# Reordering the TensorE stages of a round in a fused retention and adapter kernel

## The chip, the cores and the metric

The kernel runs on one core of one Trainium2 chip. The metric is device microseconds of one execution, lower is better. A core has five engines that each run their own list of instructions in order: TensorE (PE) for matmuls, VectorE (DVE), ScalarE (ACT), GpSimd (POOL) and SyncE (SP), which here issues nearly all transfers. [...]

## The reference

Two layers follow each other. The first is retention over q, k, v of shape (8 batches, 8 heads, 576 positions, 64): scores with a decay that depends on the distance, a causal mask, and the product with v.

```
scores = scale * matmul(q, k.transpose(0, 1, 3, 2))
ret    = scores * Dmat            # gamma_h ** (i - j) for i >= j, else 0
x      = matmul(ret, v)           # then (B, H, S, D) -> (B * S, H * D) = (4608, 512)
```

The second adds low-rank adapters to x: logits over 8 experts choose the two best for each token; their softmax weights scale the products with A (512 x 16 for each expert) and B (16 x 512).

```
logits = x @ w_gate               # (4608, 8), the top 2 chosen
delta += w * ((x @ A[e]) @ B[e])  # for the two chosen experts e
out    = x + delta
```

## The kernel before, in words

**Units.** The 576 positions are cut into four chunks of 128 and a last one of 64. A unit is one chunk of two batches (or the last chunk of four batches): units 0 to 15 are full, 16 and 17 hold the last chunk. A unit has 128 tokens in each of its two halves b. The decay is folded into q and k (scale_, on GpSimd, L166), and what earlier chunks contribute comes as a 64 x 64 state for each head, kept in the tiles blk.

**Stages of a unit on TensorE**, with the names that the profile shows for their outputs:

- T (L252): transposes of k (pt_k) and q (pt_q); evict_T copies them to kT and xq.
- SL and S (L355, L379): scores. S (ps_s) holds the first 64 keys against 128 queries, SL (a, L369) the second 64 keys against the second 64 queries. VectorE masks them: mask_e (L400) writes S's scores over xq, mask_l (L414) writes SL's to sl.
- U (L432): state products of k and v, in the other half of the tile a; add_state (L452) adds the old state.
- X (L464) and XL (L511): x, transposed, in the two banks px; X takes the masked S and the state, XL (the "late part") the masked SL. evict_x (L533) copies both to xT on ScalarE.
- Z (L563): x times the joined A and w_gate (pz). routing_1 copies it to zs on ScalarE, routing_2 finds the two best on VectorE, routing_3 makes the weights with two sigmoids on ScalarE (sg), routing_4 makes the weighted zc on GpSimd (cm, zc).
- P (L545): transposes zc (pzt); evict_z copies it to zT.
- B (L629): transposes xT into the banks po. Y (L656): adds zT times B to po. evict_o (L673) copies po to osb, which SP stores.

**Rounds.** The loop at L870 runs one round for each t from 3 on, and works on three units at a time: t, p = t - 1 and z = t - 2, besides the transposes of nxt = t + 1. The schedule is written out by hand: every engine works in the order in which the statements stand. A round of the kernel before gives TensorE SL(t), S(t), XL(p), U(t), X(p), the k transposes of nxt, B(z), the q transposes of nxt, P(z), Z(p), Y(z). So x of a unit is made one round after its scores. The rounds of t = 0 to 2 are written out ahead of the loop (L788 to L867), the work that is left after the last round stands behind it (L906 on).

**Banks.** The tiles in PSUM have tags. "s" and "a" are two banks each, "x0", "x1", "o0" and "o1" one each, which makes eight. In a round, "s" holds ps_s and then pt_k; "a" holds SL's and U's results and then pt_q; "x0" and "x1" hold px, then pz (x0) and pzt (x1); "o0" and "o1" hold po. A tag's next tile is written when the last one has been read.

**Transfers.** While clock["on"] holds, on_pe (L119) adds up an estimated duration of every matmul, and hangs the round's loads (of unit t + 3) and stores (of unit t - 3) on TensorE's instructions at set distances. The order of the engines' own work does not depend on these estimates.

Of the kernel before, what the change touches and what calls it, by code (L numbers as in the profile page):

```python
# [10 lines left out]
FP32 = mybir.dt.float32  # L11
# [7 lines left out]
def kernel(  # L19
# [441 lines left out]
                nc.vector.tensor_tensor(out=dst, in0=src, in1=old, op=ALU.add)  # L461


    def stage_X(u, bs=(0, 1)):  # L464
        c, bp = units[u]
        if u == NU - 1 and "px" not in st[u]:
            pa = pp.tile([128, 2, HP, 128], FP32, tag="a", name="pa")
            st[u]["px"] = [pa[:, 0], pp.tile([128, HP, 128], FP32, tag="x1", name="px1")]
        elif "px" not in st[u]:
            st[u]["px"] = [  # L470
                pp.tile([128, HP, 128], FP32, tag=f"x{b}", name=f"px{b}") for b in range(2)
            ]
        px = st[u]["px"]
        if c == 0:

            for hp in range(HP):
                for b in bs:
                    for ho in range(2):
                        on_pe(
                            52,  # L480
                            nc.tensor.matmul(
                                px[b][hf(ho), hp, :],
                                lhsT=blk(u)[hf(b), b, 2 * hp + ho, :],
                                rhs=facing(u, b, ho)[hf(b), hp, :],
                                start=False,
                                stop=True,
                                skip_group_check=True,
                            ),
                        )
            return  # L490
        full = c < NFULL
        parts = [(0, slice(0, 128))] if full else [(t, hf(t)) for t in range(2)]
        for b in bs:
            for hp in range(HP):
                for t, qc in parts:
                    bk = blk(u if full else 4 * NFULL + 2 * bp + t)
                    for ho in range(2):
                        on_pe(
                            107 if full else 60,
                            nc.tensor.matmul(  # L500
                                px[b][hf(ho), hp, qc],
                                lhsT=bk[:, b, 2 * hp + ho, :],
                                rhs=facing(u, b, ho)[:, hp, qc],
                                start=(hp == 0 and t == 0 and not full),
                                stop=True,
                                skip_group_check=True,
                            ),
                        )


    def stage_XL(u):  # L511
        px = st[u]["px"] = [
            pp.tile([128, HP, 128], FP32, tag=f"x{b}", name=f"px{b}") for b in range(2)
        ]
        sl = st[u]["sl"]
        vn, vl = nt(u, "v"), st[u]["vl"]
        for hp in range(HP):
            for b in range(2):
                for ho in range(2):
                    h, r = 2 * hp + ho, late_half(u, b)  # L520
                    on_pe(
                        29,
                        nc.tensor.matmul(  # L523
                            px[b][hf(ho), hp, 64:128],
                            lhsT=vn[64:128, b * H + h, :] if r else vl[0:64, h, :],
                            rhs=sl[hf(r), late_bank(u, b, ho), hp, :],
                            start=(hp == 0),
                            stop=False,
                            skip_group_check=True,
                        ),  # L530
                    )
# [55 lines left out]
    def routing_2(u):  # L587
        s = st[u]
        zs = s["zs"]
        m8 = mo.tile([128, 2, E], FP32, tag="m8", name="m8")  # L590
        ns = mo.tile([128, 2], FP32, tag="ns", name="ns")
        ge = mo.tile([128, 2, E], FP32, tag="ge", name="ge")
        for b in range(2):
            nc.vector.max(out=m8[:, b, :], in_=zs[:, b, ER : ER + E])  # L594
        nc.vector.scalar_tensor_tensor(
            out=ns, in0=m8[:, :, 0], scalar=-1.0, in1=m8[:, :, 1],
            op0=ALU.mult, op1=ALU.subtract,
        )
        nc.vector.tensor_tensor(
            out=ge, in0=zs[:, :, ER : ER + E],  # L600
            in1=m8[:, :, 1:2].broadcast_to((128, 2, E)), op=ALU.is_ge,
        )
        s["ns"], s["ge"] = ns, ge
# [22 lines left out]
            )  # L626
        s["zc"] = zc

    def stage_B(u, tag="o"):  # L629
        if tag == "s":  # L630
            both = st[u]["po2"] = pp.tile([128, 2, 2, HP, 64], FP32, tag="s", name="po")
            po = [both[:, ho] for ho in range(2)]
        else:
            po = [
                pp.tile([128, 2, HP, 64], FP32, tag=f"{tag}{ho}", name=f"po{ho}")
                for ho in range(2)
            ]
        for b in range(2):
            for dt in range(HP):
                for ho in range(2):  # L640
                    sl = slice(64 * ho, 64 * ho + 64)
                    on_pe(
                        29,
                        nc.tensor.matmul(  # L644
                            po[ho][:, b, dt, :],
                            lhsT=st[u]["xT"][b][sl, dt, :],
                            rhs=id64[sl, :],
                            is_transpose=True,
                            start=(dt == 0 and b == 0),
                            stop=False,  # L650
                            skip_group_check=True,
                        ),
                    )
        st[u]["po"] = po
# [83 lines left out]
    def load_jobs(u, w):  # L738
        return [(LOAD_NS, lambda b=b: load_half(u, w, b)) for b in range(2)] if u < NU else []
# [98 lines left out]
    stage_XL(1)  # L838
    stage_T(2, "q")
    evict_T(2, "q")  # L840
    stage_X(1)
    routing_2(0)
    evict_x(1)
    routing_3(0)

    place_v(2, pool2)
    scores(2)
    stage_U(2)
    add_state(2, nc.scalar)
    stage_T(3, "k", "o")  # L850
    evict_T(3, "k")
    routing_4(0)
    scale_(3, "k", (nc.gpsimd, nc.vector))
    place_v(3, pool2)
    for w in "kq":
        scale_(4, w, pool2)
    stage_Z(1, (0,))
    stage_P(0)
    evict_z(0)
    stage_Z(1, (1,))  # L860
    routing_1(1)
    stage_T(3, "q")
    evict_T(3, "q")
    stage_B(0)
    stage_Y(0)
    evict_o(0)
    routing_2(1)  # L867
    clock["on"] = True

    for t in range(3, NU):  # L870

        p, z, nxt = t - 1, t - 2, t + 1
        lk, lq, lv, out_jobs = [load_jobs(t + 3, w) for w in "kqv"] + [store_jobs(t - 3)]
        jobs += lk + lq[:1] + out_jobs[:1] + lq[1:] + out_jobs[1:] + lv
        routing_3(z)
        routing_4(z)
        scores(t)
        if nxt < NU:
            place_v(nxt, pool2)
        if t + 2 < NU:  # L880
            scale_(t + 2, "k", pool2)
            scale_(t + 2, "q", pool2)
        if is_full(p):
            stage_XL(p)
        if is_full(t):
            stage_U(t)
            add_state(t)
        stage_X(p)
        evict_x(p)
        if nxt == NU:  # L890
            break
        stage_T(nxt, "k")
        evict_T(nxt, "k")
        stage_B(z)
        stage_T(nxt, "q")
        stage_P(z)
        evict_z(z)
        evict_T(nxt, "q")
        stage_Z(p)
        routing_1(p)  # L900
        shift_q(nxt, (nc.scalar,) * 2 if t + 2 < NU else pool2)
        stage_Y(z)
        evict_o(z)
        routing_2(p)

    y, u = NU - 2, NU - 1  # L906
    clock["on"] = False
    flush()
    stage_B(z)
    stage_P(z, tag="x0")  # L910
    evict_z(z)
    for b in range(2):
        stage_X(u, (b,))
        evict_x(u, (b,))
    stage_Y(z)
    evict_o(z, True)
    jobs += store_jobs(z)
    flush()
    end_banks(y, "x")
    for b in range(2):  # L920
        stage_Z(y, (b,))
    end_route_1(y, 0)
    end_route_1(y, 1)
    end_route_2(y, 0)
    end_banks(u, "o")
    stage_Z(u, (0,))
    end_route_1(u, 0)
    end_route_2(y, 1)
    stage_Z(u, (1,))
    stage_B(y, "s")  # L930
    pe = pp.tile([128, 2, 2, 4, 128], FP16, tag="a", name="pe")
    st[y]["pzt"], st[u]["pzt"] = pe[:, :, 0, 0], pe[:, :, 1, 0]
    stage_P(y)
    end_route_1(u, 1)
    end_route_2(u, 0)
    evict_z(y)
    stage_B(u, "x")
    end_route_2(u, 1)
    stage_P(u)
    stage_Y(y)  # L940
    evict_z(u)
    evict_o(y)
    stage_Y(u, (0,))
    stage_Y(u, (1,))
    evict_o(u, True)
    for w, queues in ((y, (nc.sync,) * 2), (u, (nc.sync, nc.scalar))):
        for queue, (dst, src) in zip(queues, store_parts(w)):
# [32 lines left out]
```

## Time and profile before

| What | Value |
|---|---|
| Runs, median of 3 (lowest, highest) | 180.68 us (180.35, 184.98) |
| The profiled execution, its own time | 182.06 us |
| Its span, first to last instruction | 180.3 us |
| Mean granted TensorE clock | 0.997 |
| Rounds t = 4 to 15, together (starts at 42.36 and 153.04) | 110.68 us |
| Busy ScalarE, VectorE, GpSimd in the round from 88.70 to 97.70 | 6.54, 5.28, 6.84 us |

In the rows below, a line of the chain of waits has a start, a duration, an engine, the tile that it writes, the line of the code and a count; PE stands for TensorE. A line of a timeline has the operation and its shapes as well, and at its end, in brackets, how long the engine had been idle and what released it. "x16" are sixteen instructions of one kind, merged, and the duration is theirs together. The name behind "<-" in the brackets is inferred from semaphores, and can be wrong where several were waited for.

### The profile page before, as it was taken

Reading aid. Unit: us, or ns where it says so; the run is one execution under the profiler, and the core shown is the slowest. Engines: PE = TensorE matmul, PEld = TensorE weight load, DVE = VectorE, ACT = ScalarE, POOL = GpSimd, SP = SyncE. Lnnn points to the kernel's source line nnn. Section 1 sums busy time; section 2 is a strip of 40 time slices with the busy share of each in tenths; the row PEclk is TensorE's granted clock in tenths of the full one; section 3 lists DMA queues with packets and bytes.
Section 4 is the critical chain, followed back from the end, with each engine's and each line's share of the span. In section 5 each row is a group of like instructions: output and inputs, shape, how many; then the busy total and the mean of one; then the engine's idle time right before and its main releaser. Section 6 shows DMA issues by size and latency. Waiting matters only on the chain.

```text
span 180.3 us, 9353 instructions
## 1 busy us (share of the span) xinstructions
PE 168.9 (94%) x4135; PEld 151.8 (84%) x4135; DVE 92.8 (51%) x171; ACT 114.3 (63%) x217; POOL 116.5 (65%) x176
## 2 busy tenths in 40 slices
PE   7989999989998999999999999999999999899960
PEld 2677888879887999899999999989999999899940
DVE  0082666554656383929282819190919191715540
ACT  3524296558584767676767575757777777875460
POOL 0453675699978668686969695949495958762000
PEclk9999999999999999999999999999999999999998
DMA  6999999999998998999999998989999887803306
GB/s 142 250 249 214 255 224 235 247 249 229 258 240 203 227 231 225 252 231 232 237 224 253 257 256 195 250 215 246 235 240 255 216 220 200 284 5 122 120 0 233
DMA packets 119216, 39.01 MB, mean 216 GB/s; under 512 B 114180, under 2 KB 114564, under 8 KB 119176
## 3 DMA queue, kind: packets, MB, share of 16 engines
q1 hardware_dynamic: 118304, 37.82, 84.6%
q8 instruction: 32, 0.52, 1.2%
q10 hardware_dynamic: 728, 0.47, 0.9%
q0 software_dynamic: 144, 0.13, 0.4%
q14 instruction: 8, 0.07, 0.1%
HBM read 29.11 MB, written 9.44 MB: 214 GB/s over the span
## 4 chain that ended last, share of the span: by engine, by line
PE 63%; SPq 15%; DMA 9%; POOL 5%; issue 3%; DVE 1%; ACT 1%; POOLq 0%; ACTq 0%
PE pz L571 15%; PE px L500 12%; SPq L164 11%; PE a L442 7%; DMA q<-in_q_dram 6%; PE ps_s L390 5%; PE po L644 4%; PE pt_k L272 4%; DMA v<-in_v_dram 3%; PE a L369 3%; PE pt_q L272 3%; PE po L663 3%; PE px L523 3%; SPq L160 2%; PE pzt L552 2%
## 5 line engine op out<-in xcount | busy, mean ns | idle before, releaser
L171 POOL TENSOR_TENSOR k<-k,pack 128x512 f32<-128x512 f32 x35 | 35.9, 1043 | 11.9 <-PE pt_k L272 10.4
L541 ACT COPY xT<-px 128x512 f32<-128x512 f32 x35 | 20.2, 590 | 27.5 <-PE px L500 20.4
L571 PE MATMUL pz<-AW,xT 128*128 128x136 f32 x288 | 37.6, 283 | 0.0
L571 PEld LDWEIGHTS pz<-AW,xT 128*128 128x128 f32 x288 | 34.7, 190 | 0.2
L594 DVE MAX8 m<-zs 128x8 f32<-128x8 f32 x32 | 3.8, 161 | 55.9 <-ACT zs L584 55.9
L408 DVE TENSOR_TENSOR xq<-ps_s,pack 64x1024 f32<-64x1024 f32 x24 | 29.3, 1220 | 1.7 <-PE ps_s L390 1.3
L171 POOL TENSOR_TENSOR q<-q,pack 128x512 f32<-128x512 f32 x28 | 28.8, 1042 | 1.9 <-DMA q<-in_q_dram 1.9
L500 PE MATMUL px<-xq,blk 128*64 128x128 f32 (+1 forms) x480 | 27.3, 264 | 0.1
L500 PEld LDWEIGHTS px<-xq,blk 128*64 128x64 f32 x480 | 24.2, 137 | 0.7 <-issue 0.5
L347 POOL COPY blk<-v 64x512 f32<-64x512 f32 x32 | 19.5, 608 | 1.3
L442 PE MATMUL a<-v,k 128*64 128x64 f32 x512 | 19.1, 225 | 1.0 <-issue 0.8
L390 PE MATMUL ps_s<-xq,kT 64*64 64x128 f32 (+1 forms) x640 | 19.3, 260 | 0.0
L442 PEld LDWEIGHTS a<-v,k 128*64 128x64 f32 x512 | 16.6, 138 | 2.8 <-issue 1.5
L619 POOL TENSOR_TENSOR cm<-ge,sg 128x16 f32<-128x16 f32 x16 | 3.5, 221 | 22.8 <-DVE xq L408 17.4
L680 ACT COPY osb<-po 128x512 f32<-128x512 f32 x34 | 18.0, 581 | 0.0
L461 DVE TENSOR_TENSOR blk<-a,blk 64x512 f32<-64x512 f32 x24 | 16.4, 685 | 0.2
L390 PEld LDWEIGHTS ps_s<-xq,kT 64*64 64x64 f32 x640 | 16.0, 134 | 0.5 <-issue 0.4
L296 ACT COPY xq<-pt_q 128x1024 f32<-128x1024 f32 x16 | 16.3, 1019 | 0.3 <-PE pt_q L272 0.3
L324 ACT COPY xq<-xq 64x512 f32<-64x512 f32 x26 | 16.1, 617 | 0.6
L296 ACT COPY kT<-pt_k 128x1024 f32<-128x1024 f32 x15 | 15.2, 1014 | 1.2 <-PE pt_k L272 0.6
L272 PEld LDWEIGHTS pt_k<-pack,k 64*128 64x128 f32 x288 | 10.9, 139 | 5.5 <-issue 3.7
L272 PE MATMUL pt_k<-pack,k 64*128 64x64 f32 x288 | 13.5, 230 | 1.5 <-POOL zc L621 0.8
(68 smaller groups left out, 261.2 us busy)
## 6 DMA issues: line engine op xcount, KB each, us to landing
out_dram<-osb SPq DMA_DIRECT2D x35, 256.0 KB, 4.2
q<-in_q_dram SPq DMA_DIRECT2D x28, 256.0 KB, 4.9
k<-in_k_dram SPq DMA_DIRECT2D x26, 256.0 KB, 4.9
v<-in_v_dram SPq DMA_DIRECT2D x24, 256.0 KB, 4.7
v<-in_v_dram SPq DMA_DIRECT2D x6, 512.0 KB, 6.3
k<-in_k_dram SPq DMA_DIRECT2D x5, 512.0 KB, 6.3
q<-in_q_dram SPq DMA_DIRECT2D x4, 512.0 KB, 6.4
A_nat<-in_moe_A_dram SPq DMA_DIRECT2D x1, 256.0 KB
```

What stands on the lines that cost most here:

```text
L164: nc.sync.dma_start(out=nt(u, w), in_=rows(w, 2 * bp, 2, 128 * c, 128))
L171: engines[b].tensor_tensor(out=tl[:, b * H : b * H + H, :], in0=tl[:, b * H : b * H + H, :], in1=g[:, c, :].unsqueeze(2).broadcast_to((128 ...
L272: nc.tensor.matmul(ps[r][:, b, hp, :], lhsT=src[hf(r), b * H + 2 * hp : b * H + 2 * hp + 2, :], rhs=id64[hf(r), :], is_transpose=True, sta ...
L296: nc.scalar.copy(out=tl.rearrange("p b a t j -> p t (b a) j"), in_=st[u]["p2" + w].rearrange("p r b a j -> p r (b a) j"),)
L347: engs[b].tensor_copy(out=blk(u)[hf(b), b], in_=vn[0:64, b * H : b * H + H, :])
L390: nc.tensor.matmul(ps[hf(b), int(ho == b), hp, qc], lhsT=kT[hf(ho), b, hp, kc], rhs=qT[hf(ho), b, hp, qc], start=(hp == 0 and qc.start == ...
L408: nc.vector.tensor_tensor(out=dst, in0=src, in1=m, op=ALU.mult)
L442: nc.tensor.matmul(a[hf(1 - b), ho, 1, hp, :], lhsT=kn[:, h, :], rhs=vn[:, h, :], start=(hp == 0), stop=True, skip_group_check=True,),
L500: nc.tensor.matmul(px[b][hf(ho), hp, qc], lhsT=bk[:, b, 2 * hp + ho, :], rhs=facing(u, b, ho)[:, hp, qc], start=(hp == 0 and t == 0 and no ...
L541: nc.scalar.copy(out=dst, in_=src)
L571: nc.tensor.matmul(st[u]["pzb"][b] if "pzb" in st[u] else pz[:, b, :], lhsT=st[u]["xT"][b][:, dt, :], rhs=AW[:, dt, :], start=(dt == 0), s ...
L680: copy(out=s["osb"][:, :, :, ho, :], in_=s["po"][ho])
```

## The change

The change rewrites the order of a round and of what surrounds the loop.

- The loop starts at t = 2 instead of 3; the round written out for unit 2 goes. B(0) is done ahead of the loop. place_v(2) moves ahead of X(1). The scaling of k of unit 3, which GpSimd and VectorE shared, is GpSimd's alone and stands behind place_v(3).
- TensorE's order in a round becomes S(t), SL(t), P(z), Z(p), Y(z), k transposes of nxt, q transposes of nxt, B(p), U(t), X(t), XL(t). So x of unit t is made in round t itself, and the late part comes after X and not before it. The flags that start an accumulation move from XL to X.
- evict_x(t) is the last statement of a round; routing_3 and routing_4 of z stay the first two of the next.
- B(p) is done one round before Y takes the same banks, so "o0" and "o1" are held across the end of a round.
- The transposes of k go to "x0" and "x1", those of q to "s". evict_T of k and evict_o are shared by ScalarE and VectorE.
- mask_l stands behind evict_o(z) on VectorE, and routing_2(p) behind mask_l.
- Behind the loop the order of the last units changes: Z(16) ahead of X(17), B(16) and P(16) ahead of Z(17), and B(17) in the banks "s" and "a".

```diff
+    def banks_x(u):
+        if "px" in st[u]:
+            return False
+        if u == NU - 1:
+            st[u]["px"] = [
+                pp.tile([128, 2, HP, 128], FP32, tag=tg, name="px")[:, 0] for tg in "as"
+            ]
+        else:
             st[u]["px"] = [
                 pp.tile([128, HP, 128], FP32, tag=f"x{b}", name=f"px{b}") for b in range(2)
             ]
+        return True
+
+    def stage_X(u, bs=(0, 1)):
+        c, bp = units[u]
+        first = banks_x(u) or bs[0] > 0
...
-                                start=False,
+                                start=(hp == 0 and first),
...
-                                start=(hp == 0 and t == 0 and not full),
+                                start=(hp == 0 and t == 0 and first),
...
     def stage_XL(u):
-        px = st[u]["px"] = [
-            pp.tile([128, HP, 128], FP32, tag=f"x{b}", name=f"px{b}") for b in range(2)
-        ]
-        sl = st[u]["sl"]
+        first = banks_x(u)
+        px, sl = st[u]["px"], st[u]["sl"]
...
-                            start=(hp == 0),
-                            stop=False,
+                            start=(hp == 0 and first),
+                            stop=True,
...
+    def stage_B(u, tags=("o0", "o1")):
+        po = []
+        for ho, tag in enumerate(tags):
+            if tag in "sa":
+                both = pp.tile([128, 2, 2, HP, 64], FP32, tag=tag, name=f"po{ho}")
+                po.append(both[:, 0])
+            else:
+                po.append(pp.tile([128, 2, HP, 64], FP32, tag=tag, name=f"po{ho}"))
...
     stage_XL(1)
     stage_T(2, "q")
     evict_T(2, "q")
+    place_v(2, pool2)
     stage_X(1)
+    stage_B(0)
     routing_2(0)
     evict_x(1)
-    routing_3(0)
-
-    place_v(2, pool2)
-    scores(2)
-    stage_U(2)
-    add_state(2, nc.scalar)
-    stage_T(3, "k", "o")
-    evict_T(3, "k")
-    routing_4(0)
-    scale_(3, "k", (nc.gpsimd, nc.vector))
-    place_v(3, pool2)
...
-    for t in range(3, NU):
+    for t in range(2, NU):
 
         p, z, nxt = t - 1, t - 2, t + 1
+        if t > 2:
+            clock["on"] = True
...
         routing_3(z)
         routing_4(z)
-        scores(t)
-        if nxt < NU:
-            place_v(nxt, pool2)
+        stage_S(t)
+        if is_full(t):
+            stage_SL(t)
+        for b in range(2):
+            mask_e(t, b)
+        if nxt == NU:
+            break
+        stage_P(z)
+        evict_z(z)
+        stage_Z(p)
+        routing_1(p)
+        stage_Y(z)
+        evict_o(z, True)
+        if is_full(t):
+            mask_l(t)
+        routing_2(p)
+        stage_T(nxt, "k", "x")
+        evict_T(nxt, "k", True)
+        place_v(nxt, pool2)
+        if units[nxt][0] == 0:
+            scale_(nxt, "k", pool2)
         if t + 2 < NU:
             scale_(t + 2, "k", pool2)
             scale_(t + 2, "q", pool2)
-        if is_full(p):
-            stage_XL(p)
+        stage_T(nxt, "q", "s")
+        evict_T(nxt, "q")
+        stage_B(p)
+        shift_q(nxt, (nc.scalar,) * 2 if t + 2 < NU else pool2)
         if is_full(t):
             stage_U(t)
             add_state(t)
-        stage_X(p)
-        evict_x(p)
-        if nxt == NU:
-            break
-        stage_T(nxt, "k")
-        evict_T(nxt, "k")
-        stage_B(z)
-        stage_T(nxt, "q")
-        stage_P(z)
-        evict_z(z)
-        evict_T(nxt, "q")
-        stage_Z(p)
-        routing_1(p)
-        shift_q(nxt, (nc.scalar,) * 2 if t + 2 < NU else pool2)
-        stage_Y(z)
-        evict_o(z)
-        routing_2(p)
+        stage_X(t)
+        if is_full(t):
+            stage_XL(t)
+        evict_x(t)
 
     y, u = NU - 2, NU - 1
     clock["on"] = False
     flush()
-    stage_B(z)
-    stage_P(z, tag="x0")
+    stage_P(z)
     evict_z(z)
+    end_banks(y, "x")
     for b in range(2):
-        stage_X(u, (b,))
-        evict_x(u, (b,))
+        stage_Z(y, (b,))
     stage_Y(z)
     evict_o(z, True)
...
+    for b in range(2):
+        stage_X(u, (b,))
+        evict_x(u, (b,))
+        end_route_2(y, b)
+    stage_B(y)
...
     stage_P(y)
-    end_route_1(u, 1)
-    end_route_2(u, 0)
     evict_z(y)
-    stage_B(u, "x")
-    end_route_2(u, 1)
-    stage_P(u)
+    end_banks(u, "x")
+    for b in range(2):
+        stage_Z(u, (b,))
+        end_route_1(u, b)
+    for b in range(2):
+        end_route_2(u, b)
     stage_Y(y)
+    evict_o(y, True)
+    stage_B(u, ("s", "a"))
+    stage_P(u, tag="x0")
     evict_z(u)
-    evict_o(y)
-    stage_Y(u, (0,))
-    stage_Y(u, (1,))
+    stage_Y(u)
     evict_o(u, True)
```

More of the change, by code (lines that the diff above doesn't have):

```diff
@@ L461, in add_state @@
                 nc.vector.tensor_tensor(out=dst, in0=src, in1=old, op=ALU.add)
[L464 to L469, printed above, removed]
+    def banks_x(u):
[6 more added lines that the diff above has]
+        else:
             st[u]["px"] = [
@@ L627, in routing_4 @@
         s["zc"] = zc
[L629 to L637, printed above, removed]
+    def stage_B(u, tags=("o0", "o1")):
[6 more added lines that the diff above has]
+                po.append(pp.tile([128, 2, HP, 64], FP32, tag=tag, name=f"po{ho}"))
         for b in range(2):
@@ L840 @@
     evict_T(2, "q")
+    place_v(2, pool2)
     stage_X(1)
+    stage_B(0)
     routing_2(0)
     evict_x(1)
-    routing_3(0)
-    place_v(2, pool2)
-    scores(2)
-    stage_U(2)
-    add_state(2, nc.scalar)
-    stage_T(3, "k", "o")
-    evict_T(3, "k")
-    routing_4(0)
-    scale_(3, "k", (nc.gpsimd, nc.vector))
-    place_v(3, pool2)
[L855 to L868, printed above, removed]
-    for t in range(3, NU):
+    for t in range(2, NU):
         p, z, nxt = t - 1, t - 2, t + 1
-        lk, lq, lv, out_jobs = [load_jobs(t + 3, w) for w in "kqv"] + [store_jobs(t - 3)]
-        jobs += lk + lq[:1] + out_jobs[:1] + lq[1:] + out_jobs[1:] + lv
+        if t > 2:
+            clock["on"] = True
+            lk, lq, lv, out_jobs = [load_jobs(t + 3, w) for w in "kqv"] + [store_jobs(t - 3)]
+            jobs += lk + lq[:1] + out_jobs[:1] + lq[1:] + out_jobs[1:] + lv
         routing_3(z)
         routing_4(z)
-        scores(t)
-        if nxt < NU:
-            place_v(nxt, pool2)
+        stage_S(t)
[19 more added lines that the diff above has]
+            scale_(nxt, "k", pool2)
         if t + 2 < NU:
@@ L918 @@
     flush()
-    end_banks(y, "x")
-    for b in range(2):
-        stage_Z(y, (b,))
     end_route_1(y, 0)
     end_route_1(y, 1)
[L924 to L932, printed above, removed]
+    for b in range(2):
[3 more added lines that the diff above has]
+    stage_B(y)
+    st[y]["pzt"] = pp.tile([128, 2, 2, 4, 128], FP16, tag="a", name="pzt")[:, :, 0, 0]
     stage_P(y)
-    end_route_1(u, 1)
-    end_route_2(u, 0)
     evict_z(y)
-    stage_B(u, "x")
-    end_route_2(u, 1)
-    stage_P(u)
+    end_banks(u, "x")
[4 more added lines that the diff above has]
+        end_route_2(u, b)
     stage_Y(y)
+    evict_o(y, True)
+    stage_B(u, ("s", "a"))
+    stage_P(u, tag="x0")
     evict_z(u)
-    evict_o(y)
-    stage_Y(u, (0,))
-    stage_Y(u, (1,))
+    stage_Y(u)
     evict_o(u, True)
```

## The prediction, made before the changed kernel ran

> **What bounds the kernel now.** I read the page first: how long TensorE is busy, and the clock that it was granted.
>
> ```profile
> span 180.3 us, 9353 instructions
> ...
> PE 168.9 (94%) x4135; PEld 151.8 (84%) x4135; DVE 92.8 (51%) x171; ACT 114.3 (63%) x217; POOL 116.5 (65%) x176
> ...
> PEclk9999999999999999999999999999999999999998
> ```
>
> No other engine is above 65%, and TensorE's clock is full until the last slice. Then the chain of work that ended last, over round t = 9:
>
> ```profile
> 88.79 0.62 PE a L369 x32
> 89.42 0.88 PE ps_s L390 x32
> 90.29 0.46 PE px L523 x32
> 90.75 1.08 PE a L442 x32
> 91.84 1.75 PE px L500 x32
> 93.59 0.65 PE pt_k L272 x16
> 94.23 0.50 PE po L644 x16
> 94.73 0.50 PE pt_q L272 x16
> 95.23 0.22 PE pzt L552 x2
> 95.45 1.91 PE pz L571 x16
> 97.36 0.44 PE po L663 x4
> ```
>
> Eleven stages of TensorE follow each other with no hole: late scores, scores, late part, state products, x, k transposes, B, q transposes, P, Z, Y, together 9.01 us. In this round nothing but TensorE's own work sets the pace. From the timeline of TensorE, the stages that begin rounds 4, 16 and 17:
>
> ```profile
> 42.36 0.70 PE L369 MATMUL a<-xq,kT 64*64 64x64 f32 x32
> 153.04 1.16 PE L390 MATMUL ps_s<-xq,kT 64*64 64x64 f32 x64
> 161.27 1.16 PE L390 MATMUL ps_s<-xq,kT 64*64 64x64 f32 x64
> ```
>
> Rounds 4 to 15 take 153.04 - 42.36 = 110.68 us, which is 12 x 9.01 = 108.12 and 2.56 us of small hiccups; round 16 takes 8.23, and 19.03 remain from the start of round 17 to the end of the span. So the time is TensorE's work plus any hole that the order leaves in it. The change neither adds nor removes a matmul. The whole question is whether the new order leaves holes.
>
> **The change part by part: the steady round.** The new order on TensorE is S(t), SL(t), P(z), Z(p), Y(z), k transposes, q transposes, B(p), U(t), X(t), XL(t). A stage that follows full-height matmuls costs some 0.16 more (0.62 for the late scores after Y, 0.46 for the equally large late part after scores). Such places are as many as before (k transposes after Y, XL after X), so the work of a round stays 9.01: 0.88 + 0.46 + 0.22 + 1.91 + 0.44 + 0.65 + 0.50 + 0.50 + 1.08 + 1.75 + 0.62.
>
> What moves is P(z). Before, it stood some 6.4 us into the round (88.79 to 95.23); now it stands 0.88 + 0.46 = 1.34 us into it. It needs zc(z), which GpSimd makes from sg(z) (routing_4), and sg(z) is ScalarE's (routing_3), queued in the new code behind evict_x(p), the last statement of the round before, which now waits for the end of XL(p). Durations of that chain, from the timelines of ScalarE, GpSimd and TensorE:
>
> ```profile
> 25.17 1.07 ACT L541 COPY xT<-px 128x512 f32<-128x512 f32 x2
> 91.10 0.49 ACT L609 ACTIVATE sg<-zs,ns 128x8 f32<-128x8 f32 x2
> 95.28 2.07 PE L571 MATMUL pz<-AW,xT 128*128 128x136 f32 x16
> 93.64 0.59 ACT L541 COPY xT<-px 128x512 f32<-128x512 f32 x1 [0.29 <-PE px L500]
> 91.67 0.22 POOL L619 TENSOR_TENSOR cm<-ge,sg 128x16 f32<-128x16 f32 x1 [1.85 <-DVE xq L408]
> 91.97 0.76 POOL L621 TENSOR_TENSOR zc<-zs,cm 128x128 f16<-128x128 f32 x2
> ```
>
> In the chain x ends at 91.84 + 1.75 = 93.59 and its second copy starts at 93.64, 0.05 later. Counted from the end of XL(p), which is the start of S(t) in the chain: the copies start at 0.05; two back to back take 1.07 (1.12); two sigmoids 0.49 (1.61). The sigmoid row ends at 91.59 and cm starts at 91.67, so 0.08 more (1.69); cm to zc is 0.30 (1.99), zc 0.76 (2.75). GpSimd's wait of 1.85 is put down to VectorE there, but it ended as the sigmoid did. From zc to TensorE I have one place where P really waited, round 3:
>
> ```profile
> 37.22 1.07 ACT L541 COPY xT<-px 128x512 f32<-128x512 f32 x2 [2.88 <-PE px L481]
> 39.04 0.77 POOL L621 TENSOR_TENSOR zc<-zs,cm 128x128 f16<-128x128 f32 x2
> 39.50 0.59 PE L552 MATMUL pzt<-ident,zc 128*128 128x128 f16 x2
> 39.92 2.07 PE L571 MATMUL pz<-AW,xT 128*128 128x136 f32 x16
> ```
>
> The second zc ends at 39.81 and Z's row begins at 39.92: 0.11 later (2.86). A row of Z starts 0.17 ahead of its piece in the chain (95.28 against 95.45), so in the chain's time Z(p) begins 3.03 us into the new round, where without the wait it would begin at 1.34 + 0.22 = 1.56. The hole is 1.47 us in every round. Behind the waiting P the rest of TensorE's round is queued; ScalarE's copy of zT, the loads hung on TensorE, and all of the next round wait with it. Bounds: with no gap at all between the instructions Z could start at 1.07 + 0.49 + 0.22 + 0.76 = 2.54 (hole 0.98); with single copies of 0.59 and 0.2 more at one hand-over at 3.34 (hole 1.78). I take 1.47, whose gaps are all read from rows.
>
> Second new wait: the k transposes of the next unit now go to the x banks, of which x0 holds pz until routing_1 has copied it.
>
> ```profile
> 97.45 0.39 ACT L584 COPY zs<-pz 128x272 f32<-128x272 f32 x1 [0.68 <-PE pz L571]
> ```
>
> This copy ends at 97.84, 0.48 after Z (97.36), and Y covers 0.44 of it: with 0.05 to wake TensorE a hole of 0.1 a round (0 to 0.25).
>
> Third: X(t) takes the x banks as soon as the k transposes are copied out, half of that by VectorE, queued behind a half of evict_o(z), mask_l(t) and routing_2(p).
>
> ```profile
> 88.86 0.24 DVE L594 MAX8 m<-zs 128x8 f32<-128x8 f32 x2 [3.55 <-ACT zs L584]
> 89.85 0.68 DVE L422 TENSOR_TENSOR sl<-a,pack 128x512 f32<-128x512 f32 x1
> 167.68 0.69 DVE L680 COPY osb<-po 128x512 f32<-128x512 f32 x1 [2.64 <-PE po L663]
> ```
>
> VectorE needs 0.69 + 0.68 + 0.99 (88.86 to 89.85) + 0.69 = 3.05 us from Y's first half on, 2.85 after Y's end, 3.1 with a wake-up. TensorE has 0.10 + 0.65 + 0.50 + 0.50 + 1.08 = 2.83 us until X, and the bank that VectorE clears is the second batch's, touched after half of X, at 3.7. Costed at nothing, with 0.6 to spare; gone, each 0.1 beyond that is 0.1 a round. mask_l ends about 1.2 after Y, U starts 1.75 after it: nothing. B(p) held across the round: its banks are empty by then (copies of 0.6 to 0.7 after Y, B 1.25 after it): nothing. Masks now also wait for SL, which reads the q that they overwrite: P, Z, Y, both transposes, B and U cover them before X: nothing. GpSimd's copies and scalings and SP's loads and stores keep their number and order, spread over a longer round; their cover is that added time.
>
> A steady round is thus 9.01 + 1.47 + 0.10 = 10.58. [...] Rounds 4 to 15: 12 x 10.58 + 1.0 = 128.0 against 110.7, **+17.3**.
>
> **The first rounds.** The new loop begins at t = 2.
>
> ```profile
> 24.03 1.17 PE L481 MATMUL px<-xq,blk 64*64 64x128 f32 x32
> 27.48 0.22 POOL L619 TENSOR_TENSOR cm<-ge,sg 128x16 f32<-128x16 f32 x1
> 32.39 0.61 POOL L345 COPY vl<-v 64x512 f32<-64x512 f32 x1 [2.85 <-DMA v<-in_v_dram]
> 33.04 1.26 POOL L347 COPY blk<-v 64x512 f32<-64x512 f32 x2
> 34.73 2.04 POOL L171 TENSOR_TENSOR k<-k,pack 128x512 f32<-128x512 f32 x2 [0.43 <-DMA k<-in_k_dram]
> ```
>
> X(1) ends near 25.2, B(0) near 25.7, S(2) and SL(2) near 27.0. cm(0) starts at 27.48 as before (behind place_v(2)), zc ends 1.06 later, Z(1) starts at 28.65 by its row, 28.8 in the chain's time. From there 1.91 + 0.44 + 0.10 + 0.65 + 0.50 + 0.50 + 1.08 + 1.1 + 0.46 = 6.7: S(3) at 35.5. GpSimd cannot follow: v of unit 3 lands no sooner than 32.39, its copies end at 34.30, and the scaling of k(3), half of it VectorE's and ahead of v before, now stands behind them on GpSimd, followed by k(4) and q(4): 3 x 2.05 = 6.15, so 40.5. Only then comes routing_4(1): zc at 41.56, Z(2) at 41.8, where TensorE was ready at 37.1: a hole of 4.7. With 6.7 more and 0.3 for VectorE's copy (this unit's x takes both banks at once) S(4) starts at 48.8, against 42.36: **+6.4** (+4 with the k(3) scaling hidden, +8 if TensorE restarts slowly).
>
> **The end.** Round 16: Z at 3.03 again, then 1.91 + 0.44 + 0.10 + 0.65 + 0.50 + 0.50 + 2.02 for x makes 9.15 against 8.23: **+0.9**. After S(17) the chain before held these two stages, which the new order has already done:
>
> ```profile
> 162.43 2.02 PE px L500 x64
> 164.44 0.64 PE po L644 x16
> ```
>
> That is 2.66 less, but P(15) waits 1.6, and the last B and Y now stand behind both units' routing; followed in the same way the last copies end some 0.3 earlier: **-0.3** (-1.7 to +1.5).
>
> Sum: 6.4 + 17.3 + 0.9 - 0.3 = +24.3. The profiled execution took 182.06 us (span 180.3 and 1.76 around it), 0.8% above the median of 180.68; the sum on the median gives **205.0 us**.
>
> The step that carries this is that TensorE does not pass a waiting matmul. In round 3 xT was there at 38.29, yet Z started at 39.92, right after P. [...]
>
> **The rivals.**
> 1. *TensorE passes the waiting P* and runs Z(p) first, whose xT is ready at 1.12. Then 1.91 us of Z cover the hole: rounds of 9.11 and all hiccups make 111.9, round 3 loses 2.7 and not 4.7, round 16 and the end 3 us less, so +6.4 - 2 + 1.2 + 0.6 - 3: 183.9 us, within 2%. It decides where zc comes less than 1.9 us after SL. Round 3 speaks against it. 5%.
> 2. *VectorE becomes late for X.* Its four jobs have 0.6 us to spare; if sharing with GpSimd stretches them by 1 us, each round grows by 0.4 and the 12 rounds by 5: 210 us. For it: three of the four jobs are new ahead of X. Against it: the rows were taken while GpSimd was busy. 7%.
> 3. *The clock drops in the hole of round 3.* TensorE stands still for 4.7 us there; before, the only such rest is after its last matmul, in the slice that shows 8. At 0.8 for one round, its 9.01 us of work would take 2.25 longer: 207.3 us. 4%. [...]
>
> **How the numbers follow.** Forecast 84%, rivals 5, 7 and 4%. Bounds on the forecast: the hole 0.98 to 1.78 (-5.9 to +3.7), the zs wait -1.2 to +1.8, hiccups -1 to +1.6, first rounds -2.4 to +1.6, end -1.3 to +1.9. They will not all fall to one side: 197 to 211 us, which takes in rivals 2 and 3 and leaves out rival 1. About 2% (3.6 us) is what a measurement here can tell from no change. Slower by over 2%: 93%; within 2%: 5%; faster: 2%, for what I have not seen.
>
> **What would show it.** Right: each steady round has P waiting for GpSimd's zc with TensorE idle some 1.5 us, starts of S(t) about 10.6 apart, S(4) near 48.8, TensorE's share of the span near 83%. Wrong: Z(p) running before P(z), rounds near 9.1, or sg ahead of the xT copies on ScalarE. If X waits for VectorE's kT copy, rival 2 holds.

## The result, and the profile after

| | Before | Changed |
|---|---|---|
| Median of the runs | 180.82 us | 204.63 us (203.82 to 205.00, 4 runs) |
| Ratio, 95% interval | | 1.132 [1.127, 1.137] |
| Span of the profiled execution | 180.3 us | 203.2 us |
| Steady round (start of S to start of S) | 9.00 us | 10.67 us |

The changed kernel is 13% slower; 205.0 us had been forecast. Some executions of a kernel take a few per cent longer than the others (the kernel before 180.35 to 184.98 us); the ratios, here and below, are of the faster ones. The page of the changed kernel's profile:

```profile
span 203.2 us, 9353 instructions
...
PE 172.8 (85%) x4135; PEld 153.1 (75%) x4135; DVE 120.3 (59%) x203; ACT 100.0 (49%) x198; POOL 117.5 (58%) x177
...
PEclk9999999979999999999999999999999999999997
```

TensorE has the same 4135 instructions, and is busy for 85% of a longer span. One slice away from the end, the ninth, shows a 7 for the clock. The chain that ended last, in a steady round:

```profile
83.03 0.76 POOL zc L626 x2
83.84 0.23 PE pzt L557
84.07 1.92 PE pz L576 x16
86.07 0.40 ACT zs L589
86.51 0.72 PE pt_k L272 x16
```

Where the chain of round 9 before held nothing but TensorE, it now goes through GpSimd (zc) into P, and through ScalarE (zs) into the k transposes. In several other rounds the chain goes back from zc to a load of v (10% of the span in all), though the bracket of cm names the sigmoids (sg) there too; experiment 1, which moves no load, settles which of the two it was. The timelines of TensorE, ScalarE and GpSimd in round 5:

```profile
59.51 1.06 PE L390 MATMUL ps_s<-xq,kT 64*64 64x128 f32 x32
62.15 0.59 PE L557 MATMUL pzt<-ident,zc 128*128 128x128 f16 x2 [1.12 <-POOL zc L626]
62.58 2.07 PE L576 MATMUL pz<-AW,xT 128*128 128x136 f32 x16
65.18 0.72 PE L272 MATMUL pt_k<-pack,k 64*128 64x64 f32 x16
70.18 1.05 PE L390 MATMUL ps_s<-xq,kT 64*64 64x128 f32 x32
...
59.73 1.08 ACT L546 COPY xT<-px 128x512 f32<-128x512 f32 x2 [1.64 <-PE px L528]
60.83 0.49 ACT L614 ACTIVATE sg<-zs,ns 128x8 f32<-128x8 f32 x2
...
61.40 0.22 POOL L624 TENSOR_TENSOR cm<-ge,sg 128x16 f32<-128x16 f32 x1 [3.48 <-ACT sg L614]
61.70 0.76 POOL L626 TENSOR_TENSOR zc<-zs,cm 128x128 f16<-128x128 f32 x2
```

Read it from the bottom: zc ends at 62.46 and Z starts at 62.58. Before that, cm had waited 3.48 us for the sigmoids; they had stood behind the copies of xT; and ScalarE had been idle for 1.64 us ahead of those copies, since XL had not ended. The brackets name the whole chain, and the 1.64 us are time in which the sigmoids could have run.

Round 3, from the timelines of GpSimd and TensorE, and the granted clock right behind (the row of the windows view has the stretch, its length, the engines' busy times, the clock, the DMA share and GB/s):

```profile
31.64 0.61 POOL L345 COPY vl<-v 64x512 f32<-64x512 f32 x1 [3.28 <-DMA v<-in_v_dram]
39.93 0.76 POOL L626 TENSOR_TENSOR zc<-zs,cm 128x128 f16<-128x128 f32 x2
...
40.38 0.65 PE L557 MATMUL pzt<-ident,zc 128*128 128x128 f16 x2 [3.73 <-POOL zc L626]
40.83 3.35 PE L576 MATMUL pz<-AW,xT 128*128 128x136 f32 x16
```

```profile
40.50:44.50 4.00, 3.93 (x22) 3.55 (x21) 0.07 (x1) 0.60 (x2) 3.77 (x6) 0.63 1.08 246
59.50:70.20 10.70, 9.36 (x248) 8.53 (x241) 7.05 (x11) 5.68 (x11) 6.87 (x10) 1.00 0.99 249
```

After 3.73 us at rest TensorE's clock is 0.63, and Z takes 3.35 us where it takes 2.07 in round 5. In round 5, with 1.12 us of rest, the clock is whole (1.00).

The rows that begin round 16 and 17, and the copies of xT and the wait of P at the end, from TensorE and ScalarE:

```profile
176.81 1.11 PE L390 MATMUL ps_s<-xq,kT 64*64 64x64 f32 x64
186.13 1.16 PE L390 MATMUL ps_s<-xq,kT 64*64 64x64 f32 x64
188.15 0.59 PE L557 MATMUL pzt<-ident,zc 128*128 128x128 f16 x2 [0.85 <-POOL zc L626]
...
185.32 0.65 ACT L546 COPY xT<-px 128x512 f32<-128x512 f32 x1 [0.57 <-PE px L508]
```

### The profile page after: what moved, and what is told of

The parts are those of the page before. It is cut to its first block, busy times and chain, and to the rows that moved or that the text cites. A ratio compares the mean times of both kernels' runs of the same rounds, so it can differ in the third digit from the quotient of the medians.

```text
span 203.2 us, 9353 instructions
## 1 busy us (share of the span) xinstructions
PE 172.8 (85%) x4135; PEld 153.1 (75%) x4135; DVE 120.3 (59%) x203; ACT 100.0 (49%) x198; POOL 117.5 (58%) x177
## 4 chain that ended last, share of the span: by engine, by line
PE 44%; POOL 19%; DMA 14%; issue 11%; ACT 5%; SPq 3%; DVE 1%; POOLq 0%; ACTq 0%; DVEq 0%
PE pz L576 14%; DMA v<-in_v_dram 10%; PE px L508 7%; POOL k L171 6%; PE a L442 5%; POOL zc L626 5%; PE pt_k L272 4%; POOL q L171 3%; PE pt_q L272 3%; POOL blk L347 3%; PE po L648 3%; ACT zs L589 2%; PE ps_s L390 2%; PE pzt L557 2%; DMA A_nat<-in_moe_A_dram 2%
## 5 line engine op out<-in xcount | busy, mean ns | idle before, releaser
L171 POOL TENSOR_TENSOR k<-k,pack 128x512 f32<-128x512 f32 x36 | 36.8, 1044 | 11.7 <-PE pt_k L272 9.1
L576 PE MATMUL pz<-AW,xT 128*128 128x136 f32 x288 | 38.9, 289 | 0.0
L576 PEld LDWEIGHTS pz<-AW,xT 128*128 128x128 f32 x288 | 36.1, 197 | 0.1
L684 DVE COPY osb<-po 128x512 f32<-128x512 f32 x18 | 12.4, 691 | 24.0 <-PE po L667 24.0
L557 PE MATMUL pzt<-ident,zc 128*128 128x128 f16 x36 | 8.2, 232 | 21.5 <-POOL zc L626 19.3
L557 PEld LDWEIGHTS <-zc 128*128 128x128 f16 x36 | 3.4, 96 | 26.1 <-POOL zc L626 25.7
L390 PE MATMUL ps_s<-xq,kT 64*64 64x128 f32 (+1 forms) x640 | 20.2, 260 | 0.3 <-issue 0.3
L565 ACT COPY zT<-pzt 128x256 f16<-128x256 f16 x18 | 6.7, 372 | 27.7 <-PE pzt L557 27.7
L589 ACT COPY zs<-pz 128x272 f32<-128x272 f32 x16 | 6.2, 386 | 25.6 <-PE pz L576 25.6
L442 PE MATMUL a<-v,k 128*64 128x64 f32 x512 | 18.4, 225 | 0.0
L324 ACT COPY xq<-xq 64x512 f32<-64x512 f32 x26 | 16.1, 618 | 0.7
```

What stands on the lines that cost most here:

```text
L171: engines[b].tensor_tensor(out=tl[:, b * H : b * H + H, :], in0=tl[:, b * H : b * H + H, :], in1=g[:, c, :].unsqueeze(2).broadcast_to((128 ...
L324: getattr(engs[b], o)(out=st[u]["x2"][hf(1 - b), b], in_=st[u]["qT"][hf(b), b])
L390: nc.tensor.matmul(ps[hf(b), int(ho == b), hp, qc], lhsT=kT[hf(ho), b, hp, kc], rhs=qT[hf(ho), b, hp, qc], start=(hp == 0 and qc.start == ...
L442: nc.tensor.matmul(a[hf(1 - b), ho, 1, hp, :], lhsT=kn[:, h, :], rhs=vn[:, h, :], start=(hp == 0), stop=True, skip_group_check=True,),
L557: nc.tensor.matmul(pzt[:, b, :], lhsT=st[u]["zc"][:, b, :], rhs=ident16, is_transpose=True, start=True, stop=True,),
L576: nc.tensor.matmul(st[u]["pzb"][b] if "pzb" in st[u] else pz[:, b, :], lhsT=st[u]["xT"][b][:, dt, :], rhs=AW[:, dt, :], start=(dt == 0), s ...
```

## The experiments

The theory: the same work, in an order in which TensorE stands still, because P(z) is reached before ScalarE and GpSimd have made zc, and TensorE does not go around it. The rivals: that banks or xT, not zc, are what is late; that another move of the change costs the time; and for round 3, that its slow clock has another cause than the rest before it. The kernels ran on several chips, on which the kernel before took 184.4, 183.9 and 183.3 us (median); each ratio is to the kernel before on the same chip.

**1. The sigmoids ahead of the copies.** The changed kernel with routing_3 moved up by one statement (two runs of the same edit).

```
+    routing_3(0)              # ahead of evict_x(1), before the loop
...
-        routing_3(z)
+        routing_3(p)          # at the end of a round, ahead of evict_x(t)
```

> The changed kernel with one pair of statements turned round: the two sigmoids of routing_3 stand ahead of evict_x on ScalarE, at the end of each round. Theory (TensorE waits in order for zc, which waits for ScalarE's copies of xT): ScalarE has over 1 us free before those copies, so zc is there when SL ends, the hole of 1.5 us in each round goes, 12 rounds lose 18 us, round 16 another 1.5 and the start of the end 0.85; the wait of round 3 stays, since GpSimd causes it. 184 us, up to 186 if the small hiccups of the kernel before come back; rounds of 9.15 to 9.3. Rival (the hole is TensorE's own, from banks or from xT, and zc only the last name): time unchanged, 203 to 206 us.

> The first experiment once more (only the sigmoids ahead of the copies of xT), since its comparison was unclear: rounds of 9.16 where the changed kernel has 10.67, the hole of round 3 left in. Theory: 20 us less than the changed kernel, 1.01 to 1.03 of the kernel before.

The first comparison was unclear (median 187.65 us beside 184.36); its trace has a stretch of 1.8 us at the start, inside x of unit 1, that nothing in the profile explains. The second gave 1.018 [1.011, 1.024]. TensorE in its rounds 5 and 6:

```profile
59.09 1.06 PE L390 MATMUL ps_s<-xq,kT 64*64 64x128 f32 x32
60.54 0.28 PE L557 MATMUL pzt<-ident,zc 128*128 128x128 f16 x2
60.66 2.07 PE L576 MATMUL pz<-AW,xT 128*128 128x136 f32 x16
...
68.26 1.06 PE L390 MATMUL ps_s<-xq,kT 64*64 64x128 f32 x32
```

P has no bracket any more, and a round takes 9.17 us. One statement gives back 1.132 - 1.018 = 11 of the 13%. The hole of round 3 (3.39 us of rest) and the slow Z(2) behind it (3.45 us, the clock 0.62 from 41.00 to 45.00) are still there. This is the strongest single piece of evidence: nothing else in the order was touched.

**2. A shorter chain.** The second copy of xT goes to VectorE.

```
-            nc.scalar.copy(out=dst, in_=src)
+            (nc.vector.tensor_copy if share and b else nc.scalar.copy)(out=dst, in_=src)
...
-        evict_x(t)
+        evict_x(t, share=True)
```

> The changed kernel with the second half of evict_x given to VectorE inside the loop, so that ScalarE has one copy of xT (0.59 us) ahead of the sigmoids and not two (1.07). Theory: the chain in front of P gets 0.48 us shorter and each hole with it, 13 x 0.48 = 6.2 us, the wait of round 3 unchanged: 198.4 us, rounds of 10.2. Rival (the hole is not the length of this chain): 203 to 206 us.

1.079 [1.068, 1.089], which is 195 us where the kernel before takes 180.8: 3 less than forecast. Some 1.3 of these are round 3, behind whose hole the clock stayed whole this time (1.00 from 40.50 to 44.50, Z(2) 2.07 us), and 1.0 the end, where P(15) does not wait any more (16.1 us from S(17) to the end of the span, and not 17.1). A round:

```profile
58.10 1.05 PE L390 MATMUL ps_s<-xq,kT 64*64 64x128 f32 x32
60.25 0.59 PE L557 MATMUL pzt<-ident,zc 128*128 128x128 f16 x2 [0.64 <-POOL zc L626]
...
68.28 1.05 PE L390 MATMUL ps_s<-xq,kT 64*64 64x128 f32 x32
```

0.48 less of ScalarE's work ahead of the sigmoids, 0.48 less wait (0.64 and not 1.12), 0.49 less per round (10.18). So the hole follows the length of this chain.

**3. Z ahead of P.**

```
+        stage_Z(p)
         stage_P(z)
         evict_z(z)
-        stage_Z(p)
```

> The changed kernel with Z(p) ahead of P(z) on TensorE. Theory (TensorE does not pass a waiting matmul, so only the written order can fill the hole): Z starts right after SL, 1.91 us of it cover the wait for zc, and Y then waits some 0.5 us for ScalarE's copy of zT, which Z covered before. Rounds of 9.5, 12 x 1.15 = 13.8 us less, round 3 loses 3 us less, round 16 1.2: 186 us. If xT or the bank of pz were what is late, Z would wait as P did and the time would stay near 204.

1.043 [1.033, 1.053]: most of the loss is gone, 186 (1.03) was somewhat too low. A round:

```profile
56.73 1.06 PE L390 MATMUL ps_s<-xq,kT 64*64 64x128 f32 x32
58.18 2.12 PE L576 MATMUL pz<-AW,xT 128*128 128x136 f32 x16
...
60.88 0.61 PE L667 MATMUL po<-Bcat,zT 128*128 128x256 f16 x4 [0.47 <-ACT zT L565]
...
66.42 1.06 PE L390 MATMUL ps_s<-xq,kT 64*64 64x128 f32 x32
```

Z starts 1.45 us into the round, at once, so neither xT nor its bank was late. The wait moved to Y, as foreseen; the round takes 9.69 and not 9.5, since the hand-overs from Z through P and zT to Y cost 0.2 more than I had counted. Had TensorE passed a waiting matmul by itself, the written order would have made no difference.

**4. P early in the kernel before.** One thing of the change alone.

```
         scores(t)
         if nxt < NU:
+            stage_P(z)
+            evict_z(z)
...
-        stage_P(z)
-        evict_z(z)
```

> The kernel before with one thing of the change alone: P(z) and evict_z(z) stand right behind the scores of round t. Theory (the place of P against ScalarE's queue sets the price): sg ends 2.87 us after the start of a round there, zc 4.0, and the late part has to wait for the copy of zT as well, to 4.75 where it began at 1.4: 3.3 us in each of the rounds 4 to 16 and some 5 in round 3, 222 to 232 us. Rival (the place of P costs nothing by itself, the other moves make the loss): 180 to 184 us.

1.343 [1.331, 1.355], 247 us: the right direction, and 15 us more than the upper end. From its timeline, and the windows view of that round:

```profile
78.63 0.59 PE L552 MATMUL pzt<-ident,zc 128*128 128x128 f16 x2 [2.14 <-POOL zc L621]
...
80.73 1.97 PE L442 MATMUL a<-v,k 128*64 128x64 f32 x32
```

```profile
75.40:89.20 13.80, 11.33 (x243) 10.14 (x236) 4.97 (x10) 6.61 (x13) 6.85 (x10) 0.88 0.63 157
```

The state products take 1.97 us where they took 1.15, and the clock over the round is 0.88. The wait was forecast, the clock was not. In round 4, after the same rest of 2.14 us, it had still stayed at 1.00.

**5. The hole filled.** The fourth experiment with 8 matmuls on zeros ahead of P, in each round.

```
         if nxt < NU:
+            fill(8, "x0", 0)
             stage_P(z)
```

> The kernel before with P right behind the scores, as in the fourth experiment, and 8 matmuls on zeros in the hole ahead of P, which is 2.1 us long there; nobody reads their result. Theory (a hole of that length also halves the clock for some 3 us, which is why that experiment took more than the wait alone): granted clock near 1.00, rounds of 11.6 as its one round at full clock, 247 - 11 x 2.2 = 223 us. Rival (the added time is not the clock): rounds stay near 13.8.

229.7 us in one run (1.25 of the kernel before), 17 us less for more work, where 24 less had been forecast. The same view:

```profile
74.20:86.50 12.30, 11.67 (x239) 9.42 (x238) 4.99 (x9) 6.60 (x13) 6.85 (x10) 1.00 0.73 186
```

The clock is 1.00 in this round, as in all from 4 to 15, and the rounds take 12.3 us: that is 9.0 and the 3.3 of waiting which the fourth experiment's working gave. The other 1.5 us of its 13.8 were the clock. (The 11.6 that I had taken from its one round at full clock was a first round, shorter than the others.)

**6. The same in the changed kernel's round 3.**

```
+        if t == 3:
+            fill(14, "x0", 0)
         stage_P(z)
```

> The changed kernel with 14 matmuls on zeros, whose result nobody reads, ahead of P in round 3 alone, where TensorE stands idle for 3.7 us and the clock then falls to 0.63. Theory (the idle stretch lowers the clock): granted clock 1.00 behind it, Z(2) 2.07 us and not 3.35, 1.3 us less in all. Rival (the clock falls there for another reason): Z(2) stays near 3.3.

```profile
42.70 2.11 PE L576 MATMUL pz<-AW,xT 128*128 128x136 f32 x16
```

Z(2) takes 2.11 us, and the clock is 1.00 from 42.50 to 46.50, as the theory has it. It is one run, and in experiment 2 the clock stayed whole behind 3.53 us with nothing in the hole, so this run alone does not show that the rest lowered it; the dozen rounds of experiments 4 and 5 do, for the holes there. The total, 205.97 us, says nothing, since this run too has a stretch of 2.5 us at the start that nothing explains.

**7. GpSimd's order in round 3.**

```
         routing_4(z)
+        if t == 3:
+            scale_(3, "k", pool2)   # and no longer ahead of it, in round 2
```

> The changed kernel with the scaling of k(3) moved behind zc(1) on GpSimd, nothing else. Theory: zc(1) comes 2.0 us sooner, the hole of round 3 shrinks from 3.7 to 1.7 us idle; if 1.7 is too short for the clock to fall, another 1.3 us: 2.0 to 3.3 us less than the changed kernel, 1.114 to 1.121 of the kernel before. Rival (round 3 waits for something else): 1.13.

1.124 [1.117, 1.131], which reaches from the theory's range to the rival's 1.13, so the time is inconclusive. TensorE rested 0.99 us ahead of P in round 3, where it was 3.73, and the clock stayed at 1.00 there. But the profiled run has a stretch of 1.85 us at the start and a slow clock behind it (0.77 from 30.00 to 36.00), so that S(3) starts at 38.98 and not at 35.14: TensorE comes later, and the rest is shorter for that reason too. What the edit itself did is seen on GpSimd. There cm(1) now waits 0.92 us for the sigmoids, where in the changed kernel, and in experiment 6 with a stretch of the same kind, it follows GpSimd's own scalings at once. So it was these scalings that held up zc(1); how much time their move is worth stays open.

**8. Without the holes.** Experiment 1, with zc(1) made right after k(4) on GpSimd; then, besides, the q transposes ahead of the k transposes; then, instead of that, zc(2) early as well, and half of k(3) on VectorE. The last of the three:

```
+    routing_3(0)
     evict_x(1)
...
-        routing_3(z)
-        routing_4(z)
+        if t not in (3, 4):
+            routing_4(z)
...
-        if units[nxt][0] == 0:
-            scale_(nxt, "k", pool2)
         if t + 2 < NU:
             scale_(t + 2, "k", pool2)
-            scale_(t + 2, "q", pool2)
+            if t > 3:
+                scale_(t + 2, "q", pool2)
...
+        routing_3(p)
+        if t < 4:
+            routing_4(p)
+            scale_(t + 2, "q", pool2)
+        if t == 2:
+            scale_(3, "k", (nc.vector, nc.gpsimd))
         evict_x(t)
```

> The sigmoids ahead of the copies of xT as in the first experiment, and in round 2 GpSimd makes zc(1) right after k(4), ahead of q(4) and k(3). Theory: zc(1) is there near 37 us, so the 3.7 us hole of round 3 goes, and the slow clock behind it (1.25 us); unit 4's scores start near 44, not 48.8. Rounds of 9.16, as the first experiment showed, 12 of them 110 us, round 16 7.7, the end 16: a span of 178 to 180, 0.99 to 1.00 of the kernel before on the same chip. Rival (the new order has a loss that the holes do not explain): 1.02 or more of the kernel before.

> The kernel of the previous line with the q transposes (bank s, long free) ahead of the k transposes (bank x0, which holds pz until ScalarE has copied it). Theory: the last hole of a round, 0.15 us between Y and the transposes, goes: rounds of 9.01, 13 x 0.15 = 2 us less, 0.98 to 0.99 of the kernel before. Rival (evict_T of k comes later on ScalarE and X has to wait for its bank): no gain.

> The fifth experiment (sigmoids ahead of the copies, zc(1) early) left a hole of 1.9 us in round 4 with a slow clock behind it, since the q(4) and k(3) scalings that were put off now stood ahead of zc(2) on GpSimd. Here zc(2) too is made ahead of q(5), and half of k(3) is VectorE's again, as in the kernel before. Theory: that hole and the slow clock go, 1.9 + 1.5 = 3.4 us, rounds of 9.16 from the fourth on: 0.985 to 0.995 of the kernel before. Rival (the holes only move on, or small hiccups take the gain): 1.00 to 1.01.

The first: 1.006 [1.002, 1.010]. The hole of round 3 moved to round 4, with the slow clock behind it (0.55 from 48.87 to 52.70):

```profile
48.87 0.65 PE L557 MATMUL pzt<-ident,zc 128*128 128x128 f16 x2 [1.92 <-POOL zc L626]
49.31 3.55 PE L576 MATMUL pz<-AW,xT 128*128 128x136 f32 x16
```

The second: 1.005 [1.001, 1.009], no gain to speak of in the round (9.15). The rival held in another form: bank s, which I had called long free, is free only when VectorE has read the scores:

```profile
67.75 2.47 DVE L408 TENSOR_TENSOR xq<-ps_s,pack 64x1024 f32<-64x1024 f32 x2 [2.38 <-PE a L369]
...
69.61 0.60 PE L667 MATMUL po<-Bcat,zT 128*128 128x256 f16 x4
70.28 0.71 PE L272 MATMUL pt_q<-pack,q 64*128 64x64 f32 x16
```

The masks end at 70.22, the q transposes start at 70.28, where they would have started 0.53 after Y, at 70.14. The third: 0.999 [0.994, 1.004]. Its rounds take 9.17 us, and TensorE still rests 1.0 us in round 2 and 1.7 in round 3, but not in round 4. All three had been forecast lower than they came out, and no version beats the kernel before by anything that can be measured. Freed of most of its holes, the new order is worth as much as the old one; whether it would be worth more without the last of them, no run shows.

## Why the prediction held

| Term | Forecast | Measured |
|---|---|---|
| Start of S(4) | 48.8 | 48.8 |
| Rounds 4 to 15 | 128.0 | 128.0 |
| Round 16 | 9.15 | 9.32 |
| From S(17) to the end of the span | 18.7 | 17.1 |
| Span | 204.6 | 203.2 |

- **The hole ahead of P.** Forecast 1.47, from the links 0.05 (XL to the copies), 1.07, 0.49, 0.08, 0.30, 0.76 and 0.11 us. In round 5 the copies start 0.03 after the last row of XL (which ends at 59.70), and the links behind are 1.10, 0.49, 0.08, 0.30, 0.76 and 0.12: each is within 0.03 of its forecast. Z starts 62.58 - 59.51 = 3.07 after S, where in experiment 1, without the wait, it is 60.66 - 59.09 = 1.57. So the hole is 1.50. The bracket of P shows 1.12 of it; most of the rest lies between P and Z, which start 0.43 apart here and 0.12 apart in experiment 1. That TensorE does not pass P is shown by experiment 3, and in round 5 by Z, whose xT was there at 60.81 and which started at 62.58, behind P. That ScalarE does not run the sigmoids ahead of the copies is seen in the same round: ns, which they read, was made at 56.00, ScalarE was idle for 1.64 us up to 59.73, and they started at 60.83, behind the copies. Experiment 1, which turned the two round, took 11 of the 13% away.
- **The hole behind Y.** Forecast 0.1, measured 0.16: the k transposes start 65.18 - 62.58 = 2.60 after Z, and 1.91 + 0.53 = 2.44 of it are work (0.53 is from the start of Y to the next stage where nothing waits, 190.49 to 191.02 at the end of the same run).
- **Rounds 4 to 15.** 9.01 + 1.50 + 0.16 is the round of 10.67 that was measured, 0.09 above the forecast of 10.58. Twelve times that is 1.1 us, and nearly as much, 1.0, had been allowed for hiccups, of which none came. So the mechanism and the size of the holes were right, but that the sum agrees to a tenth is luck. What the hiccups of the kernel before are, and why the changed kernel has none, no run shows; nor does one show the 1.0, which was my estimate: in its place the twelve rounds took 10.67 each, with nothing on top.
- **X behind VectorE's copy** was costed at nothing, and no wait of X appears: it starts 0.98 us after U and its row takes 1.92, in round 5 (66.83, 67.81) as in round 9 before (90.69, 91.67). VectorE's four jobs took 3.30 us in round 5 (64.91 to 68.21), where 3.05 had been counted. Rival 2 fell.
- **Round 3** came out right by errors that cancel, which is luck as well. GpSimd got v of unit 3 at 31.64 and not 32.39, so zc(1) ended at 40.69 and not 41.56, and the 0.3 us allowed for VectorE's copy were not needed. But the clock fell, to which I had given 4%: Z(2) took 1.28 us longer. What rival 3 describes was there, at a smaller price than the 2.25 us estimated for it. The +8 of the first rounds, for a slow restart, was my estimate; the 1.28 us are what was measured.
- **Rival 1** (TensorE passes P) fell by the trace of round 5 and by experiment 3.
- **The end** is the term that was mis-sized, by 1.6 us: I let P(15) wait 1.6 and it waited 0.85. Unit 16 has no late part, so the first half of its x is copied while the second is still being made (185.32, with S at 186.13), and the sigmoids come sooner. And the later B and Y of the last units, to which the forecast's -0.3 leaves some 0.8 (-0.3 + 2.66 - 1.6), cost nothing on top: 19.03 - 2.66 + 0.85 = 17.2.

## What to carry to other kernels

When a stage is moved up in an in-order queue, walk back from it through every engine's queue and ask what stands ahead of its input there: here a 0.49 us pair of sigmoids behind two copies cost 1.5 us in each round, with 1.6 us of the same engine idle just before. If the moved order does the same work on the engine that sets the pace, its gain is at most the holes that the old one had; in its twelve rounds the old one had 2.56 us, so there was little to win and much to lose. And where an engine stands idle, waiting for another one, as ScalarE did for 1.64 us ahead of the copies, look first for a small instruction queued behind that wait which could run ahead of it.

## What the runs showed of the hardware

The clock fell after rests shorter than the 4.7 us of rival 3, and not each time. After 1.12 us of rest in each round (changed kernel) it stayed at 1.00. It fell after 3.73 us in round 3 of the changed kernel (0.50 from 40.38 to 43.40, 1.00 again from 43.60 to 48.80), after 2.13 to 2.14 us in experiment 4 from round 5 on (0.88 over a round), after 1.92 in the first kernel of experiment 8 (0.55 in the 3.8 us behind), and after 1.62 in round 2 of its second kernel (0.69 in the 4.0 us behind); but after 2.14 in round 4 of experiment 4 and in round 2 of the first kernel of experiment 8, and after 1.68 in round 3 of the third kernel there, it stayed at 1.00. In round 3 of experiment 2 it stayed at 1.00 even after 3.53 us. So behind rests of 1.6 us and more both were seen, and in three of the places where the clock fell, the rest cost 1.3 to 1.5 us more than itself (Z of 3.35 and 3.55 us and not 2.07, rounds of 13.8 and not 12.3).

What the stretches of about 2 us inside x of unit 1 are, which some of the runs have at their start and others not, stays open; the profile names no wait for them.
